# Linear attention in front of a two-layer gated network: attention sums in column halves, shorter weight split, and an engine order set by a planner

## Chip, cores and metric

One core of one Trainium2 chip runs the whole program in one launch. The metric is device time in microseconds, the median of repeated executions; lower is better.

## What is computed

```python
# attention: batch 4, heads 4, seq 1088, head_dim 32, r = 8
phi(x)[i*8+j] = (S1 @ x)[i] * (S2 @ x)[j]          # 64 features of a token and head
kv  = sum over s of phi(k[s]) x v[s]               # 64 x 32 of a batch and head
z   = sum over s of phi(k[s])
x   = (phi(q) @ kv) / (phi(q) @ z + 1e-6)          # 4352 tokens x 128 channels
# gated network: d_model 128, d_ff 2048
h = x @ w_in
g = where(h >= 1, h, where(h <= -1, 0, (h + 1)**2 / 4))
out = g @ w_out
```

The inputs are float64 or float32 arrays; the weights and S arrive as 64-bit words and are turned to float32 parts on the chip.

## The kernel before

**Network.** The 4352 tokens lie in the free dimension in 9 chunks, eight of 512 and one of 256; a *unit* is one chunk with one of 16 blocks of 128 hidden channels, 144 units in all. `up(u)` (L257) forms h in three matmuls (L262 to L264): each operand is a high part that TensorE's one-pass fp32r format holds and a low part that is the remainder, and hi·hi, hi·lo and lo·hi are summed in PSUM. ScalarE makes `s = ((h+1)/2)^2` (L270, L271), VectorE `g = min(max(h,1),s)` (L275), and once more with a rounded output as `g_hi` (L274), or ScalarE rounds a copy (L277, a share of 0.5 of the first 32 units, 0.35 later); GpSimd subtracts for `g_lo` (L278). `down(u)` (L282), four units later, adds three matmuls to the chunk's sum (L289 to L291).

**Attention.** A batch has 9 tiles of 128 tokens, in groups of 3. `features` (L155) projects a group by S (L160, plain fp32, which TensorE runs as two instructions a matmul), copies one factor (L164, ScalarE) and multiplies (L165, VectorE). `k_steps` (L172) sums keys: for each tile and pair of heads, a matmul with 128 stationary feature columns and 66 moving ones (L187: two heads' values and a column of ones for z). `q_steps` (L194) transposes the features (L206), multiplies by kv (L213: 128 stationary columns, 66 moving, which gives numerator and denominator token by token), divides (L219 to L221), and transposes x back to channels (L226) for x_hi and x_lo (L235, L236).

**Weights.** `from_double` (L76) splits 512 columns at a time, eight times: bounds (L82), magnitude (L85), bit moves (L87, L89), range test (L91), exponent (L94), low word as float (L101), its scaling (L102), rounding (L103), remainder (L104) and sum (L105).

**Order.** Attention steps come from generators in two hand-written strings (FS, SS, L26); the main loop (L344) issues as many as the next chunk needs and one more each unit, so attention runs as far ahead as one step a unit takes it. All PSUM tiles share one ring of eight banks (L54). The framework's scheduler, run with a timeline model, then orders each engine's queue.

## Time and profile before

| what | value |
|---|---|
| timed runs, median of 3 (lowest, highest) | 282.64 us (282.19, 283.64) |
| profiled execution, span (no other time of it is listed) | 423.2 us |
| its TensorE clock, mean | 0.555 of full speed |
| busy in it: PE, DVE, ACT, POOL | 418.1, 222.2, 219.5, 204.7 us |

PE is TensorE's matmuls, DVE VectorE, ACT ScalarE, POOL GpSimd, SP the engine that issues DMAs here. The page gives busy time by engine over the span, a strip of 40 slices (PEclk is the granted TensorE clock in tenths), the chain of work that ended last, and groups of instructions by line. The profiled execution ran at little over half of TensorE's clock and so took half as long again as the timed ones; a busy time of PE has to be scaled by the clock of its stretch before it is set beside the timed median, those of the other engines do not.

### The profile page before, as it was taken

The page shows a single profiled execution, that of the slowest core. Times are in us where ns is not written, and L with a number is a line of the kernel's source. Part 1 is how long each engine was busy: PE and PEld are TensorE (multiplying, and loading weights), DVE is VectorE, ACT ScalarE, POOL GpSimd, SP SyncE. Part 2 cuts the span into 40 slices and gives each one's busy share as a digit, 9 for nine tenths or more (in the row PEclk, how much of TensorE's full clock was granted, in tenths as well). Part 3 has the DMA queues.
Part 4 walks back from the last instruction along what each step waited for, and adds up shares of the span by engine and source line. Part 5 has one row for each costly group of instructions (what it writes and reads, how often), then busy time and mean ns, then how long its engine had stood idle before and what let it go on. Part 6 is the DMA issues. An engine that isn't in the chain of part 4 may idle for free.

```text
span 423.2 us, 4212 instructions
## 1 busy us (share of the span) xinstructions
PE 418.1 (99%) x1413; PEld 290.9 (69%) x1413; DVE 222.2 (53%) x390; ACT 219.5 (52%) x422; POOL 204.6 (48%) x173
## 2 busy tenths in 40 slices
PE   8999999999999999999999999999999999999997
PEld 6997877778766767786767655555555555567775
...
PEclk6555555555555555555555555555555555555555
...
GB/s 269 415 163 71 52 57 0 2 57 0 0 2 0 0 51 1 1 2 0 0 25 2 0 0 25 2 1 1 25 2 0 0 25 0 2 25 1 2 1 37
DMA packets 4629, 13.90 MB, mean 33 GB/s; under 512 B 512, under 2 KB 1152, under 8 KB 4608
## 3 DMA queue, kind: packets, MB, share of 16 engines
...
q14 instruction: 10, 0.08, 0.1%
...
## 4 chain that ended last, share of the span: by engine, by line
PE 97%; DMA 1%; DVE 0%; SPq 0%; ACT 0%; issue 0%; ACTq 0%
PE h L264 13%; PE h L262 13%; PE h L263 13%; PE acc L291 12%; PE acc L289 12%; PE acc L290 12%; PE kv L187 6%; PE nd L213 5%; PE tp L206 3%; PE ab_q L160 3%; PE ab_k L160 2%; PE xt L226 2%; DMA q_sb<-in_qT 1%; SPq L113 0%; DVE kp L165 0%; DVE topw L91 0%
## 5 line engine op out<-in xcount | busy, mean ns | idle before, releaser
L278 POOL TENSOR_TENSOR g_lo<-g,g_hi 128x512 fp32r<-128x512 f32 (+1 forms) x140 | 173.1, 1250 | 179.7 <-ACT g_hi L277 108.4
L270 ACT ACTIVATE s<-h 128x512 f32<-128x512 f32 (+1 forms) x144 | 82.3, 574 | 148.9 <-PE h L264 148.2
L274 DVE SCALAR_TENSOR_TENSOR g_hi<-h,s 128x512 fp32r<-128x512 f32 (+1 forms) x89 | 58.0, 651 | 95.5 <-ACT s L271 55.1
L275 DVE SCALAR_TENSOR_TENSOR g<-h,s 128x512 f32<-128x512 f32 (+1 forms) x144 | 92.8, 653 | 27.5 <-ACT s L271 26.7
L271 ACT ACTIVATE s<-s 128x512 f32<-128x512 f32 (+1 forms) x144 | 84.7, 605 | 1.3
L262 PE MATMUL h<-x_hi,wi_hi 128*128 128x512 f32 (+1 forms) x144 | 82.4, 572 | 0.4 <-ACT x_hi L235 0.4
L289 PE MATMUL acc<-g_hi,wo_lo 128*128 128x512 f32 (+1 forms) x144 | 81.4, 566 | 0.0
L264 PE MATMUL h<-x_hi,wi_lo 128*128 128x512 f32 (+1 forms) x144 | 80.6, 560 | 0.0
L291 PE MATMUL acc<-g_lo,wo_hi 128*128 128x512 f32 (+1 forms) x144 | 80.3, 565 | 0.0
L290 PE MATMUL acc<-g_hi,wo_hi 128*128 128x512 f32 (+1 forms) x144 | 79.5, 552 | 0.0
L263 PE MATMUL h<-x_lo,wi_hi 128*128 128x512 f32 (+1 forms) x144 | 79.5, 552 | 0.0
L290 PEld LDWEIGHTS acc<-g_hi,wo_hi 128*128 128x128 f32 x144 | 33.5, 232 | 17.4 <-issue 8.4
L289 PEld LDWEIGHTS acc<-g_hi,wo_lo 128*128 128x128 f32 x144 | 33.3, 231 | 17.3 <-issue 8.6
L291 PEld LDWEIGHTS acc<-g_lo,wo_hi 128*128 128x128 f32 x144 | 33.2, 232 | 16.7 <-issue 8.6
L264 PEld LDWEIGHTS h<-x_hi,wi_lo 128*128 128x128 f32 x144 | 31.2, 216 | 19.6 <-issue 12.0
L262 PEld LDWEIGHTS h<-x_hi,wi_hi 128*128 128x128 f32 x144 | 33.9, 236 | 15.5 <-issue 7.1
L263 PEld LDWEIGHTS h<-x_lo,wi_hi 128*128 128x128 f32 x144 | 32.9, 228 | 16.6 <-issue 10.4
L277 ACT CAST g_hi<-g 128x512 fp32r<-128x512 f32 (+1 forms) x55 | 32.8, 596 | 10.6 <-DVE g L275 10.6
L187 PEld LDWEIGHTS kv<-v_sb,kp 128*128 128x128 f32 x144 | 30.3, 298 | 2.4 <-issue 0.8
L213 PEld LDWEIGHTS nd<-kv_sb,qpT 128*128 128x128 f32 x144 | 29.1, 289 | 3.5 <-issue 1.5
L187 PE MATMUL kv<-v_sb,kp 128*128 128x66 f32 x144 | 29.1, 363 | 0.0
L213 PE MATMUL nd<-kv_sb,qpT 128*128 128x66 f32 x144 | 28.4, 348 | 0.0
...
## 6 DMA issues: line engine op xcount, KB each, us to landing
...
```

The costliest lines, as they stand in the source:

```text
L187: nc.tensor.matmul(kv[:, p * VC : (p + 1) * VC], lhsT=kp[:, t, p * P : (p + 1) * P], rhs=v_sb[:, t, p * VC : (p + 1) * VC], start=(t == 0) ...
L213: nc.tensor.matmul(nd[:, c : c + VC], lhsT=qpT[:, p, i * P : (i + 1) * P], rhs=kv_sb[b][:, p].rearrange("p h c -> p (h c)"), start=True, s ...
L262: nc.tensor.matmul(h[:, :n], lhsT=wi_hi[:, fj], rhs=x_hi[:, :n], start=True, stop=False)
L263: nc.tensor.matmul(h[:, :n], lhsT=wi_hi[:, fj], rhs=x_lo[:, :n], start=False, stop=False)
L264: nc.tensor.matmul(h[:, :n], lhsT=wi_lo[:, fj], rhs=x_hi[:, :n], start=False, stop=True)
L270: nc.scalar.activation(s[:, :n], h[:, :n], AF.Relu, bias=0.5, scale=0.5)
L271: nc.scalar.activation(s[:, :n], s[:, :n], AF.Square)
L275: nc.vector.scalar_tensor_tensor(out=g[:, :n], in0=h[:, :n], scalar=1.0, in1=s[:, :n], op0=ALU.max, op1=ALU.min)
L278: (nc.vector if u >= len(units) - 4 else nc.gpsimd).tensor_tensor(out=g_lo[:, :n], in0=g[:, :n], in1=g_hi[:, :n].bitcast(F32), op=ALU.subt ...
L289: nc.tensor.matmul(acc[:, :n], lhsT=wo_lo[:, fj], rhs=g_hi[:, :n], start=(j == 0), stop=False)
L290: nc.tensor.matmul(acc[:, :n], lhsT=wo_hi[:, fj], rhs=g_hi[:, :n], start=False, stop=False)
L291: nc.tensor.matmul(acc[:, :n], lhsT=wo_hi[:, fj], rhs=g_lo[:, :n], start=False, stop=(j == NJ - 1))
```

## The change

It does five things.

1. *Column halves.* Key sums (new L423) take 64 columns of v as stationary operand and 128 feature columns as moving one, and write PSUM partitions 0 to 63 for one pair of heads and 64 to 127 for the other. Numerators (new L497) take 64 columns of the transposed kv as stationary and up to 384 tokens as moving operand, again into two halves. x so comes out channel by channel, and the transposes of L226 go.
2. *Denominator.* z is summed as an 8x8 matrix a head from the factors (new L406), masked (L411) and multiplied into S2 (L413, L415), so that the query projection gets 32 further columns (L452: 96 instead of 64). VectorE forms the denominator from them (L460, L464), inverts it (L466) and scales one query factor by it (L469) before the features are formed (L473).
3. *Weights by bits.* The low word's three bits are shifted into the float32 pattern (new L332), which replaces L94, L101, L102 and L105 for the weights; GpSimd takes six of the eight bounds (L306).
4. *Buffers.* PSUM is split into rings of 4 (h), 2 (attention) and 2 (sums); x_hi and x_lo are whole arrays.
5. *Order.* Each step states a due unit, an engine (or two), a cost, what it reads and writes; `Plan.run` plays the engines forward in time by these costs, each taking the ready step with the earliest due, none more than 9 units ahead of the earliest step still open, and the framework keeps that order. Attention of a batch is due just before its first chunk.

```diff
-    ps = ctx.enter_context(tc.tile_pool(name="ps", bufs=8, space=PSUM))
+    rings = dict(h=4, at=2, acc=2, k=2, q=2, v=2, raw=3, hc=2, mag=3, m=2, low=1, ab=2, kp=1, as_=2, den=2,
+                 ap=2, qp=2, qpT=4, kvm=1, kvb=2, zm=1, s=4, g=4, g_hi=6, g_lo=6, o=2)
+    ctx.enter_context(tc.manual_schedule())
...
-        nc.vector.tensor_scalar(out=m, in0=top.bitcast(I32), scalar1=-0x00800000, scalar2=None,
-                                op0=ALU.bitwise_and)
-        nc.scalar.activation(low, lw.bitcast(U32), AF.Copy, scale=2.0**-52)
-        nc.gpsimd.tensor_tensor(out=low, in0=low, in1=m.bitcast(F32), op=ALU.mult)
-        nc.scalar.copy(dst_hi, top)
-        nc.gpsimd.tensor_tensor(out=top, in0=top, in1=dst_hi.bitcast(F32), op=ALU.subtract)
-        nc.gpsimd.tensor_tensor(out=dst_lo, in0=top, in1=low, op=ALU.add)
+        plan.either(due, [("DVE", fast(n), None, [raw_tok], [hc], lambda: bound(nc.vector)),
+                          ("POOL", 0.1 + 0.0016 * n, None, [raw_tok], [hc], lambda: bound(nc.gpsimd))])
+        plan.add(due, "DVE", dve(n), lambda: nc.vector.scalar_tensor_tensor(
+            out=of(m), in0=lw(), scalar=29, in1=of(m),
+            op0=ALU.logical_shift_right, op1=ALU.bitwise_or), r=[raw_tok], w=[m])
+        plan.add(due, "POOL", pool_t(n), lambda: nc.gpsimd.tensor_tensor(
+            out=lo, in0=of(mag), in1=hi.bitcast(F32), op=ALU.subtract), r=[mag, toks[0]], w=[toks[1]])
...
-                nc.tensor.matmul(kv[:, p * VC : (p + 1) * VC], lhsT=kp[:, t, p * P : (p + 1) * P],
-                                 rhs=v_sb[:, t, p * VC : (p + 1) * VC], start=(t == 0), stop=(t == NTL - 1))
+                    nc.tensor.matmul(of(kv)[64 * p : 64 * p + 64, :P], lhsT=of(vb)[:, t, 64 * p : 64 * p + 64],
+                                     rhs=of(kp)[:, t, p * P : (p + 1) * P], start=(t == 0), stop=(t == NTL - 1))
+                    nc.tensor.matmul(of(z)[:HR, :HR], lhsT=of(sbuf)[:, 1, m], rhs=of(sbuf)[:, 0, m],
+                                     start=(t == 0), stop=(t == NTL - 1))
...
-                nc.tensor.matmul(nd[:, c : c + VC], lhsT=qpT[:, p, i * P : (i + 1) * P],
-                                 rhs=kv_sb[b][:, p].rearrange("p h c -> p (h c)"), start=True, stop=True)
-        nc.vector.tensor_scalar(out=den[:, :m], in0=ndv[:, :, D:], scalar1=1e-6, scalar2=None, op0=ALU.add)
-        nc.vector.reciprocal(out=den[:, :m], in_=den[:, :m])
-        nc.vector.tensor_tensor(out=x_sb[:, :n].rearrange("p t (h d) -> p (t h) d", h=H), in0=ndv[:, :, :D],
-                                in1=den[:, :m].broadcast_to([P, m, D]), op=ALU.mult)
-            nc.tensor.transpose(out=xt[:, i * P : (i + 1) * P], in_=x_sb[:, i, :], identity=ident)
+                    nc.tensor.matmul(of(abc)[:, i * 96 : (i + 1) * 96], lhsT=of(qb)[:, t], rhs=pr, start=True, stop=True)
+                out=terms[ti][:, :m, :R], in0=of(a)[:, :m], in1=view()[:, :, 2], op=ALU.mult),
+                out=of(den)[:, :m], in_=terms[ti][:, :m], axis=AX.X, op=ALU.add), r=[("terms", ti)], w=[den])
+                out=of(ap)[:, :m], in0=view()[:, :, 0], in1=of(den)[:, :m].broadcast_to([P, m, R]), op=ALU.mult),
+                    nc.tensor.matmul(of(nd)[64 * p : 64 * p + 64, :nt], lhsT=of(kvb)[:, 64 * p : 64 * p + 64],
+                                     rhs=of(qpT[p])[:, :nt], start=True, stop=True)
...
-    for u in range(len(units)):
-        while ready < c0 + n:
-            advance()
-        up(u)
-        advance()
-        if u >= LAG:
-            down(u - LAG)
+                for s, v, ready in todo[e]:
+                    if s.taken is not None or ready > now + 1e-9 or (e != "SP" and s.due > limit):
+                        continue
+                    k = (s.due, sid[s])
+                    if best is None or k < best[0]:
+                        best = (k, s, v)
+            dues.append(lambda f, e=first_of[c] - 4, l=10: e - l + l * f)
+    order = plan.run()
+    for s in order:
+        s.ways[s.taken][5]()
```

How it moves instructions. First TensorE's queue from the first projection to the first unit (h0): `ab_k`/`abk` and `ab_q`/`abq` are projections of keys and queries of a batch and group, `tp` transposed features, `nd` numerators. Before, from L160 on:

```order
L160 MATMUL ab_k0_6_140<-s_sb_108,k_sb0_94 128x64 x3
L160 MATMUL ab_q0_0_148<-s_sb_108,q_sb0_98 128x64 x3
...
L187 MATMUL kv0_171<-v_sb0_99,kp0_125 128x66 x13
L206 MATMUL tp0_0_0_183<-ident_73,qp0_0_147 128x128 x3
...
L213 MATMUL nd0_1_240<-kv_sb0_172,qpT0_1_203 128x66 x5
L226 MATMUL xt0_0_259<-ident_73,x0_0_235 128x128 x3
...
L226 MATMUL xt0_1_278<-ident_73,x0_1_247 128x128 x3
L262 MATMUL h0_318<-x_hi0_263,wi_hi_121 128x512
```

Now:

```order
L390 MATMUL abk0_2_158<-s_all_92,k0_106 128x64 x3
L406 MATMUL z0_150<-ab0_1_156 32x32 x3
L423 MATMUL kv0_172<-kp0_148,v0_121 64x128 x6
...
L413 MATMUL z0_150<-zm0_191,s_all_92 128x32
...
L452 MATMUL abq0_0_212<-proj0_93,q0_110 128x96 x3
...
L483 MATMUL tp0_0_1_262<-ident_66,qp0_0_251 128x128 x3
L497 MATMUL nd0_0_274<-qpT0_0_0_266,kvb0_236 64x384
L497 MATMUL nd0_0_274<-qpT0_0_1_270,kvb0_236 64x384
...
L390 MATMUL abk1_0_313<-s_all_92,k1_146 128x64 x5
L539 MATMUL h0_327<-x_hi_89,wi_hi_85 128x512
```

The query projections have moved behind the key sums and behind z, 12 numerator matmuls have become 4, and no transposes stand between the numerators and h0.

Then the place on TensorE where attention ends, the last group of batch 3. Before, it stands between units 57 and 60 of 144:

```order
L264 MATMUL h58_1834<-x_hi1536_967,wi_lo_122 128x512
L213 MATMUL nd3_2_1819<-kv_sb3_1331,qpT3_2_1748 128x66 x5
L226 MATMUL xt3_1_1847<-ident_73,x3_1_1777 128x128 x3
L262 MATMUL h59_1856<-x_hi1536_967,wi_hi_121 128x512
...
L226 MATMUL xt3_2_1869<-ident_73,x3_2_1826 128x128 x3
L262 MATMUL h60_1882<-x_hi1536_967,wi_hi_121 128x512
```

Now:

```order
L541 MATMUL h105_2528<-x_hi_89,wi_lo_86 128x512
L578 MATMUL acc3072_2392<-g_lo101_2478,wo_hi_87 128x512
L497 MATMUL nd3_1_2538<-qpT3_1_0_2486,kvb3_1985 64x384
L497 MATMUL nd3_1_2538<-qpT3_1_1_2513,kvb3_1985 64x384
L574 MATMUL acc3072_2392<-g_hi102_2498,wo_hi_87 128x512
L575 MATMUL acc3072_2392<-g_hi102_2498,wo_lo_88 128x512
L497 MATMUL nd3_2_2551<-qpT3_2_0_2494,kvb3_1985 64x320
L497 MATMUL nd3_2_2551<-qpT3_2_1_2520,kvb3_1985 64x320
```

The last numerators have moved from unit 58 to unit 105, so that attention lies among 105 units rather than 59.

## Rows read from the trace of the kernel before

**Rows 1.** The page: span, busy time by engine, and the granted clock by slice.

```profile
span 423.2 us, 4212 instructions
PE 418.1 (99%) x1413; PEld 290.9 (69%) x1413; DVE 222.2 (53%) x390; ACT 219.5 (52%) x422; POOL 204.6 (48%) x173
PEclk6555555555555555555555555555555555555555
```

**Rows 2.** Busy time by stretch: start and end, length, then busy us and instructions of PE, weight loads, DVE, ACT and POOL, the granted clock, DMA share, GB/s.

```profile
0.00:33.50 33.50, 31.61 (x141) 28.34 (x141) 18.12 (x36) 11.46 (x26) 7.16 (x14) 0.57 0.72 272
33.50:60.00 26.50, 26.44 (x106) 22.00 (x106) 24.30 (x37) 16.01 (x34) 19.39 (x16) 0.54 0.22 66
60.00:100.00 40.00, 40.00 (x147) 29.70 (x148) 23.18 (x38) 21.62 (x41) 24.55 (x20) 0.55 0.05 15
100.00:140.00 40.00, 40.00 (x144) 28.44 (x142) 22.19 (x40) 17.98 (x34) 19.29 (x15) 0.56 0.00 0
140.00:180.00 40.00, 40.00 (x150) 29.16 (x148) 19.21 (x34) 19.75 (x36) 15.29 (x12) 0.56 0.04 14
180.00:220.00 40.00, 40.00 (x144) 28.35 (x144) 20.03 (x38) 18.02 (x33) 15.24 (x12) 0.56 0.02 7
220.00:260.00 40.00, 40.00 (x129) 26.01 (x128) 20.51 (x40) 20.96 (x38) 15.52 (x13) 0.56 0.00 0
260.00:300.00 40.00, 40.00 (x105) 22.73 (x104) 19.65 (x33) 23.87 (x43) 24.95 (x20) 0.56 0.02 7
300.00:340.00 40.00, 40.00 (x106) 22.79 (x105) 18.09 (x30) 23.39 (x42) 21.79 (x18) 0.56 0.04 14
340.00:380.00 40.00, 40.00 (x113) 23.73 (x112) 17.01 (x29) 22.46 (x43) 20.44 (x17) 0.56 0.02 7
380.00:423.20 43.20, 40.06 (x146) 29.66 (x144) 19.93 (x42) 24.02 (x56) 21.03 (x21) 0.56 0.03 10
```

**Rows 3.** TensorE's matmuls in order of time: start us, us, then the instructions merged; plain fp32 matmuls are two instructions each.

```profile
4.48 3.69 PE L160 MATMUL ab_k<-s_sb,k_sb 128*128 128x64 f32 x18
8.64 4.10 PE L160 MATMUL ab_q<-s_sb,q_sb 128*128 128x64 f32 x18 [0.47 <-DMA q_sb<-in_qT]
12.54 5.76 PE L187 MATMUL kv<-v_sb,kp 128*128 128x66 f32 x26
20.76 2.13 PE L206 MATMUL tp<-ident,qp 128*128 128x128 f32 x9
33.56 0.79 PE L262 MATMUL h<-x_hi,wi_hi 128*128 128x512 f32 x1 [0.35 <-ACT x_hi L235]
...
250.79 0.56 PE L264 MATMUL h<-x_hi,wi_lo 128*128 128x512 f32 x1
251.19 0.56 PE L262 MATMUL h<-x_hi,wi_hi 128*128 128x512 f32 x1
```

**Rows 4.** Groups by line, engine and shape: count, busy us, mean ns, idle time before and its releasers.

```profile
L94 DVE TENSOR_SCALAR mw<-topw 128x512 int32<-128x512 int32 x8 | 6.1, 757 | 0.0
L221 DVE TENSOR_TENSOR x<-nd,den 128x384 f32<-128x384 f32 x12 | 6.7, 556 | 0.3
L219 DVE TENSOR_SCALAR den<-nd 128x12 f32<-128x12 f32 x12 | 2.0, 170 | 13.2 <-PE nd L213 13.0
L236 DVE TENSOR_TENSOR x_lo<-xt,x_hi 128x64 fp32r<-128x64 f32 x4 | 0.9, 216 | 0.0
L236 DVE TENSOR_TENSOR x_lo<-xt,x_hi 128x128 fp32r<-128x128 f32 x3 | 0.9, 284 | 0.0
L274 DVE SCALAR_TENSOR_TENSOR g_hi<-h,s 128x512 fp32r<-128x512 f32 x77 | 53.0, 688 | 93.8 <-ACT s L271 53.5 <-PE acc L290 27.1 <-ACT g_hi L277 5.4
L277 ACT CAST g_hi<-g 128x512 fp32r<-128x512 f32 x51 | 31.2, 612 | 10.3 <-DVE g L275 10.3
L101 ACT ACTIVATE loww<-raw_i 128x512 f32<-128x512 uint32 x4 | 2.7, 663 | 0.0
L102 POOL TENSOR_TENSOR loww<-loww,mw 128x512 f32<-128x512 f32 x8 | 10.2, 1281 | 28.9 <-DVE mw L94 28.9
L104 POOL TENSOR_TENSOR topw<-topw,wi_hi 128x512 f32<-128x512 f32 x4 | 5.1, 1279 | 0.0
L105 POOL TENSOR_TENSOR wi_lo<-topw,loww 128x512 fp32r<-128x512 f32 x4 | 5.8, 1442 | 0.2
```

**Rows 5.** Single lines of VectorE's weight work: count, then shortest, median and longest duration in ns.

```profile
L82 DVE TENSOR_SCALAR hcw<-raw_i x4: 418/419/1500, 12.6 to 53.5; 128x512 f32<-128x512 f32 x4
L89 DVE SCALAR_TENSOR_TENSOR mw<-hcw,mw x8: 679/1086/1655, 13.8 to 101.5; 128x512 int32<-128x512 int32 x8
```

**Rows 6.** Stretches between changes of the granted clock, columns as in Rows 2.

```profile
7.20:24.20 17.00, 16.53 (x79) 16.34 (x79) 8.01 (x13) 5.61 (x14) 2.32 (x2) 0.50 1.02 405
34.50:51.50 17.00, 17.00 (x73) 13.88 (x73) 16.23 (x26) 11.43 (x23) 10.96 (x9) 0.56 0.22 67
51.60:58.40 6.80, 6.80 (x25) 6.03 (x25) 5.82 (x9) 2.61 (x7) 5.81 (x6) 0.50 0.29 89
95.90:99.30 3.40, 3.40 (x13) 2.81 (x13) 1.19 (x2) 1.74 (x3) 3.00 (x3) 0.50 0.00 0
```

**Rows 7.** TensorE just before and in the stretch from 51.60, columns as in Rows 3.

```profile
47.72 4.68 PE L187 MATMUL kv<-v_sb,kp 128*128 128x66 f32 x24
52.20 1.48 PE L160 MATMUL ab_q<-s_sb,q_sb 128*128 128x64 f32 x6
```

More of the change, by code (lines that the diff above doesn't have):

```diff
@@ L241, in woven @@
[L241 to L254 removed]
+    x_hi = cst.tile([P, NT], F32R, name="x_hi")
+    x_lo = cst.tile([P, NT], F32R, name="x_lo")
@@ new lines, in tile_kernel, with heat, emit, load @@
+    SC = S.shape[1]
+    s_raw = cst.tile([P, SC, 2], I32, name="s_raw")
+    s_all = cst.tile([P, SC], F32, name="s_all")
+    proj = [cst.tile([P, H, 3 * R], F32, name=f"proj{i}") for i in range(2)]
+    def heat(due, n):
+        b = bank(f"heat{due}", "h")
+        def emit():
+            for _ in range(n):
+                nc.tensor.matmul(of(b), lhsT=ones[:, :P], rhs=ones, start=True, stop=True)
+        plan.add(due, "PE", n * 0.43, emit, w=[b])
+    def load(due, src, b, size, tok=None, view=lambda t: t):
+        plan.add(due, "SP", 0.5, lambda: nc.sync.dma_start(view(of(b)) if isinstance(b, Buf) else view(b), src),
+                 w=[tok or b], lat=size / 410e3)
@@ new lines, in unit @@
+        plan.add(u, "DVE", dve(n), lambda: clamp(g), r=[h, s], w=[g])
+        if int((u + 1) * 0.36) > int(u * 0.36):
+            plan.add(u, "ACT", act(n, False), lambda: nc.scalar.copy(of(g_hi)[:, :n], of(g)[:, :n]), r=[g], w=[g_hi])
+        else:
+            plan.add(u, "DVE", dve(n), lambda: clamp(g_hi), r=[h, s], w=[g_hi])
+        late = u >= len(units) - 4
+        eng = nc.vector if late else nc.gpsimd
+        plan.add(u, "DVE" if late else "POOL", dve(n) if late else pool_t(n), lambda: eng.tensor_tensor(
+            out=of(g_lo)[:, :n], in0=of(g)[:, :n], in1=of(g_hi)[:, :n].bitcast(F32), op=ALU.subtract),
+            r=[g, g_hi], w=[g_lo])
@@ new lines, in tile_kernel @@
+    heat(-30, 9)
+    load(-30, S, s_raw, P * SC * 8, tok="s_raw")
+    load_attn(0, -29, -28, -27)
+    from_double(-25, lambda: s_raw, "s_raw", SC, "s", whole=s_all, whole_tok="s_all")
+    for i in range(2):
+        plan.add(-20, "ACT", act(64, False), lambda i=i: nc.scalar.copy(
+            proj[i][:, :, : 2 * R], s_all[:, :64].rearrange("p (h c) -> p h c", h=H)), r=["s_all"], w=[("proj", i)])
+    kvb = keys(0, lambda f: -16 + 7 * f)
+    queries(0, kvb, [lambda f: -9 + 4 * f, lambda f: -8 + 4 * f, lambda f: -2 + 5 * f])
@@ new lines, in tile_kernel @@
+    first_unit = {}
+    for u, (c0, n, j) in enumerate(units):
+        first_unit.setdefault(j // JW, u)
+    for c in range(DFF // WC):
+        weights(first_unit[c] - 6 if c else -10, w_in, c, wi_hi, wi_lo, "i")
+        weights(first_unit[c] - 2 if c else -6, w_out, c, wo_hi, wo_lo, "o")
+    need = {}
+    for b in range(1, B):
+        c_first = (b * SEQ) // CH * CH
+        need[b] = first_of[c_first]
+        k0 = 8 if b == 1 else need[b - 1] + 2
+        k1 = need[b] - 18
+        load_attn(b, k0 - 12, k0 - 8, k0 - 10)
+        kvb = keys(b, lambda f, k0=k0, k1=k1: k0 + (k1 - k0) * f)
+        dues = []
+        for gi in range(len(GRP)):
+            tok = b * SEQ + GRP[gi][0] * P
+            c = tok // CH * CH
+            dues.append(lambda f, e=first_of[c] - 4, l=10: e - l + l * f)
+        queries(b, kvb, dues)
```

654 lines of the change are left out of this document (413 added, 241 removed).

## The prediction

> **What bounds the kernel now.** I read the page first, then busy time by stretch, then TensorE in order of time, then the groups by line. In the profiled execution TensorE is busy 418.1 of 423.2 us, and its granted clock stays by the lower of its two levels, 1.2 of 2.4 GHz (mean 0.555) [rows 1]. Nothing else matters there. But the timed median is 282.64, so the timed runs cannot have had that clock: TensorE's 418.1 us at 0.555 are 232 us at the full clock, and to end in 282.64 it needs a mean of at least 232/282.64 = 0.82. I therefore read the profile for durations, scale TensorE's by its clock and leave the others as they are. The profiled span is half as long again as the median, and the sum below is made twice: for the timed clock, which the forecast is for, and for the profiled one, as a check.
>
> At the full clock TensorE is no longer alone. Of each stretch the reader is to take the longest of PE busy x PEclk, DVE, ACT and POOL [rows 2]. From 33.5 to 60 it is DVE (24.3 us, against PE's 26.44 x 0.54 = 14.3), to 100 POOL (24.6), over the four 40 us stretches to 260 PE (40 x 0.555 = 22.2 each; in the first DVE has as much), then POOL (25.0), ACT (23.4, 22.5, 24.0). Their sum is 232.5. PE alone makes 213.9 of these 390 us (14.3 + 22.0 + 320.06 x 0.555), DVE 204.1, ACT 208.1, POOL 197.5. So 18.6 us of the floor are unevenness: while weights and attention are made DVE is full, later it idles and ACT and POOL are full.
>
> The first 33.5 us I keep as they are, since there the clock was at 0.50 although TensorE was busy 16.53 of 17 us [rows 6]: that stretch does not look like one that the timed clock would shorten. With it the floor is 266.0; the median stands 16.6 above, so the part behind the front takes 249.1/232.5 = **1.071** times its floor. That is waiting by order. (If the front did shorten to some 22 us in the timed runs, the factor would be 1.12, and the forecast would come out within 2 us of what follows.)
>
> **TensorE.** Its plain fp32 instructions cost their stationary columns plus twice their moving ones, one after the other: key sums took 5.76/26 = 0.22 us at the lower level, 266 cycles, for 128 + 132 columns; projections 3.69/18 = 0.205, or 246, for 128 + 128; transposes 2.13/9 = 0.24 [rows 3]. At the full clock, over the whole kernel: key sums, 144 instructions of 260 cycles, are 15.6 us; as 144 of 64 + 256 they are 19.2 one after another and 9.6 if the two halves run side by side. Numerators were 15.6 too; as 32 instructions of 64 + 768 and 16 of 64 + 640 cycles they are 15.8, or 7.9 side by side. 36 transposes of x go (-3.8). Query projections gain 64 cycles in 72 instructions (+1.9), z adds 72 of some 96 cycles (+2.9), masks and transposed kv some 0.5. Side by side: -6.0 - 7.7 - 3.8 + 5.3 = **-12.2**; one after another **+5.3**. The trace has no half-width matmul, so both ends stay; I take side by side, because in the network a 512-column matmul starts every 0.40 us with its 128-column load hidden [rows 3], so TensorE does overlap work of neighbouring instructions where they don't need the same cells. Three quarters fall behind the front: -9.2, so PE 204.7 (or 217.9).
>
> The Trainium skill (TensorE: Matmul & The Clock Gate, part 3) says that a weight load overlaps running matmuls only when the row group differs; both halves here use all rows, and by that rule the sum would be nearer the second end. The same part tells of three column tiles running 2.38 times as fast, which is the first end; no run here shows either yet.
>
> **VectorE.** Removed: eight L94 (6.1), six bounds of 0.42 (2.5), L219 (2.0), L221 (6.7) [rows 4, 5]; x in whole groups saves seven x_lo pieces and nine casts with 1536 columns, by 0.216 us at 64 and 0.284 at 128 columns some 0.15 an instruction and 0.00106 a column [rows 4]: 4.0; three fewer key products 0.5. Together -21.8. Added: eight L332 on 512 integers, like L89, 0.68 to 1.66, median 1.09 [rows 5]: 8.7; 36 small instructions of 96 columns, between 0.216 and 0.284, at 0.25: 9.0; g_hi six times more at 512, twice less at 256: 3.3; S with 192 columns and masks: 2. Together +23.0. Net **+1.2** (ends -2 and +6): 205.3 behind the front.
>
> **ScalarE and GpSimd.** ACT loses eight L101 of 0.66 (5.3) and a net 2.9 of roundings (0.612 each), gains 1.6 of x_hi and 2.5 of small copies: **-4.1**, 204.0. POOL's 24 weight instructions of 1.28 to 1.44 become 8 [rows 4], -21; six bounds come, for which no row exists, between DVE's 0.42 and POOL's 1.28, at 1.1: +6.6; **-14**, 183.5. A POOL instruction beside DVE's is not free: the same bound took DVE 0.42 or 1.50 us [rows 5]; that is inside DVE's upper end.
>
> **DMA.** S grows threefold, q and v of batch 0 come in thirds; total bytes hardly change, and behind the first 60 us the DMA share is at most 0.05 [rows 2], so it costs only the 1 us in S's chain, below.
>
> **Front.** Before, h0 starts at 33.56 [rows 3]. Now TensorE has before h0, at the lower level: keys 18 x 0.205 = 3.7, z 36 x 0.08 = 2.9, key sums 36 x 0.267/2 = 4.8, queries 18 x 0.267 = 4.8, 12 transposes 2.8, 8 numerator instructions of 0.69, halved, 2.8, ten projections of batch 1 2.1: 23.9. It starts about 1 us later than 4.48, since seven instructions on S have three times the columns. 29.4, so I take 29. What is late next is the chain of small VectorE instructions ahead of the transposes; it lies beside the key sums of the same batch only in part, and two more us there are in the range.
>
> **Order.** Attention now ends at unit 105, not 58. PE, DVE and ACT then have 204.7, 205.3 and 204.0: perfectly even, the floor would be 205.3, with the old unevenness 223.9. I take the middle, 214.6, since weights must still be made early, where DVE was full (16.23 of 17 us [rows 6]). With the old factor, 214.6 x 1.071 + 29 = **259**; the two ends 249 and 269. At the profiled clock TensorE alone counts: 423.2 - 4.5 - 9.2/0.555 = 402.
>
> **Rivals.**
> 1. *The halves take turns.* PE behind the front 217.9, front 36.6: (217.9 + 9.3) x 1.071 + 36.6 = 280. For it: in plain fp32 load and matmul already run one after the other [rows 3]. Chance 0.13.
> 2. *Each change of shape empties the array.* The new queue changes stationary width 55 times, 42 of them behind the front. A matmul of 0.56 us with the next start after 0.40 [rows 3] has 0.16 still to run; 42 x 0.16 = 6.7 on PE: (211.4 + 9.3) x 1.071 + 31 = 267. The Trainium skill (TensorEngine Tiling (Array Packing), key properties) says that changing the tiling mode drains TensorE; no run here shows it. Chance 0.11.
> 3. *The clock: slower.* After 24 instructions of key sums and six of projections the clock stood at 0.50 for 6.8 us, network matmuls included [rows 6, 7]. Attention behind the front comes in 15 groups (9 of queries, 6 of keys), in half-width matmuls. If each brought 6.8 us at the lower level in a run that otherwise has the upper, PE would need 15 x 3.4 = 51 more: 255.7 x 1.071 + 29 = **303**. It passes 282.64 from 9.4 of the 15 groups on ((282.64 - 29)/1.071 - 204.7 = 32). Against it: behind 34.5 us the old kernel, with 18 such groups, fell twice [rows 6], and the new ones are shorter. Chance 0.09; some other hold-up of a fixed queue, 0.04.
> 4. *The planner does not even out.* 269, with the other gains whole. Chance 0.11.
> 5. *The planner also removes the waits.* 214.6 + 29 = 244, or 234 if even too. Chance 0.12.
>
> **The numbers.** The forecast itself, 249 to 269, has 0.40. What is within 0.5% (281.2 to 284.1) can hardly be told from no change. Faster are the forecast, rivals 2, 4, 5 and half of rival 1: 0.79; slower rival 3, the other hold-up and a third of rival 1: 0.17; the rest 0.04. The range 240 to 281 leaves out rival 3, the low half of rival 5 and the top of rival 1, some 0.2.
>
> **What would show it.** Key sums and numerators: pairs at half their single cost, starts of two halves overlapping. First h about 29 us. Behind the front DVE, ACT and PE x clock each near 205, and no 40 us stretch where one stands 3 us above the others. L332 near 1.1 us. If the granted clock is again 0.56, a span near 402 with PE at 99%; more than 425 there speaks for rival 1. The prediction is wrong at its root if the timed runs are bound by TensorE at a mixed clock: then only TensorE's -12 counts.

## The result

| | median | lowest to highest | runs |
|---|---|---|---|
| before | 283.14 us | 282.19 to 284.93 | 4 |
| after | 274.68 us | 273.26 to 277.12 | 4 |

Ratio 0.969, 95% interval 0.962 to 0.976: faster by 8.5 us, 3.1%. The forecast was 259.0 in 240 to 281. The sign and the range held; of the 23.6 us it promised, about a third came.

The profiled execution of after ran at the full clock behind its front, unlike that of before, so the two pages can't be laid side by side. Its page (span, busy time, granted clock) answers to [rows 1]:

```profile
span 272.7 us, 4152 instructions
PE 256.7 (94%) x1365; PEld 196.8 (72%) x1365; DVE 218.0 (80%) x386; ACT 207.6 (76%) x418; POOL 193.2 (71%) x170
PEclk9997999999999999999999999999999999999999
```

The comparison therefore uses a second profile of the unchanged kernel before (e0 below), which had the upper level for most of its span:

```profile
span 279.6 us, 4212 instructions
PE 266.2 (95%) x1413; PEld 225.1 (81%) x1413; DVE 221.1 (79%) x390; ACT 210.1 (75%) x422; POOL 207.3 (74%) x173
PEclk9757978999999999999999999999999999999999
```

The kernel before was bound by TensorE at the full clock as well: 95% busy. Its busy time is not the 232 us that scaling [rows 1] gave, but 266. Busy time by stretch of after (columns as in [rows 2]) shows where TensorE is the bound and where it isn't:

```profile
20.00:30.00 10.00, 8.35 (x36) 5.09 (x37) 9.03 (x17) 4.59 (x11) 2.33 (x3) 0.83 0.21 57
30.00:40.00 10.00, 9.32 (x44) 6.20 (x42) 10.00 (x15) 9.65 (x22) 7.79 (x6) 1.00 0.18 58
40.00:60.00 20.00, 17.51 (x114) 13.16 (x114) 20.00 (x29) 13.65 (x27) 16.89 (x12) 1.00 0.51 192
60.00:80.00 20.00, 17.00 (x78) 12.02 (x76) 20.00 (x33) 15.48 (x31) 15.97 (x12) 1.00 0.02 6
80.00:100.00 20.00, 20.00 (x109) 15.82 (x108) 18.37 (x33) 17.16 (x34) 17.69 (x14) 1.00 0.15 52
100.00:140.00 40.00, 40.00 (x215) 30.62 (x214) 28.41 (x50) 32.68 (x62) 28.75 (x23) 1.00 0.03 10
...
180.00:220.00 40.00, 40.00 (x193) 31.83 (x192) 33.49 (x63) 35.47 (x68) 32.93 (x27) 1.00 0.04 14
```

From 80 us on TensorE is full, with VectorE, ScalarE and GpSimd below it. From 30 to 80 VectorE is full while weights are split, and TensorE has 6.2 us of idle time. The second profile of before, the same stretches:

```profile
30.00:40.00 10.00, 6.97 (x39) 5.86 (x39) 9.06 (x14) 5.97 (x14) 7.32 (x6) 0.89 0.24 81
40.00:60.00 20.00, 20.00 (x110) 17.28 (x110) 20.00 (x30) 14.89 (x31) 16.69 (x13) 0.88 0.19 61
60.00:80.00 20.00, 19.54 (x118) 16.35 (x117) 19.96 (x34) 16.40 (x33) 19.82 (x14) 1.00 0.09 30
80.00:100.00 20.00, 18.57 (x111) 15.87 (x111) 19.27 (x34) 13.28 (x26) 20.00 (x16) 1.00 0.00 1
```

**What a matmul costs.** The ends of matmuls are modelled in the profile and hide gaps, so I go by their starts. After, in order of time (columns as in [rows 3]): network matmuls, then a burst of key sums and a group of numerators.

```profile
92.17 0.39 PE L574 MATMUL acc<-g_hi,wo_hi 128*128 128x512 f32 x1
92.39 0.39 PE L575 MATMUL acc<-g_hi,wo_lo 128*128 128x512 f32 x1
92.62 0.39 PE L539 MATMUL h<-x_hi,wi_hi 128*128 128x512 f32 x1
92.85 0.39 PE L540 MATMUL h<-x_lo,wi_hi 128*128 128x512 f32 x1
...
106.96 1.31 PE L423 MATMUL kv<-kp,v 128*64 128x128 f32 x20
108.20 0.50 PE L539 MATMUL h<-x_hi,wi_hi 128*128 128x512 f32 x1
108.54 0.40 PE L540 MATMUL h<-x_lo,wi_hi 128*128 128x512 f32 x1
...
135.79 0.39 PE L578 MATMUL acc<-g_lo,wo_hi 128*128 128x512 f32 x1
136.11 0.87 PE L497 MATMUL nd<-qpT,kvb 128*64 128x384 f32 x4
136.91 0.50 PE L574 MATMUL acc<-g_hi,wo_hi 128*128 128x512 f32 x1
```

And in the second profile of before:

```profile
33.17 0.39 PE L263 MATMUL h<-x_lo,wi_hi 128*128 128x512 f32 x1
33.40 0.40 PE L264 MATMUL h<-x_hi,wi_lo 128*128 128x512 f32 x1
33.64 0.39 PE L263 MATMUL h<-x_lo,wi_hi 128*128 128x512 f32 x1
...
118.41 2.12 PE L187 MATMUL kv<-v_sb,kp 128*128 128x66 f32 x18
120.33 0.48 PE L291 MATMUL acc<-g_lo,wo_hi 128*128 128x512 f32 x1
```

Among its like, a network matmul of 512 columns starts 0.227 us after the one before it in after and 0.232 us in before (medians at the full clock); one of 256 columns takes 0.12 in both. Why they are 4 to 5 ns further apart in before is not shown. At the full clock 512 columns alone are 512/2400 = 0.213, so 14 to 19 ns come on top of each. With 768 of the one and 96 of the other the network is **186 us** of TensorE at after's price, 190 at before's. Key sums took 1.92/18 = 0.107 us an instruction before and 1.24/20 = 0.062 now: the halves do run side by side.

Added up start to start behind the first unit (at 33.2 us before, 28.4 after), with network matmuls of both kernels at after's price (0.2275 and 0.121) and what exceeds it apart:

| us of TensorE | before | after |
|---|---|---|
| network at 0.2275 and 0.121 | 185.9 | 185.9 |
| attention | 40.9 | 34.1 |
| above the network's price: waits, returns from attention, lower clock | 16.3 | 20.6 |
| sum | 243.1 | 240.6 |

So it took 4.8 us less in the front and 2.5 less behind it: attention gave 6.8, and 4.3 of that went again into what exceeds the price. Gaps alone (the next instruction starts over 0.13 us later than the price of a network matmul, at the full clock) grew from 5.0 to 10.0 us.

The granted clock has a part in this too. Before's was at 0.50 for 6.8 us behind its first unit, from 37.8 to 44.6; the network matmuls there lie 1.8 us above their price, and 3.4 us of attention ran at half speed, some 3.5 us lost in all (an estimate from these figures). After has no such stretch. At the same clock after would have gained nothing behind the front in these two profiles: what attention gave there, the gaps took. All five profiles of before and its variants at the upper level (e0, e6, e10, e11, e12) have such a stretch; of the ten of after and its variants, eight have none but for the last 2 us, and e1 and e7 have 6.8 us.

The waits of TensorE in after from 28 to 80 us (us in total, times, longest) have one main name, VectorE:

```profile
PE acc L574 <- DVE g_hi L554: 2.3, 2, 1.4
PE h L540 <- DVE x_lo L503: 1.4, 1, 1.4
PE h L539 <- DVE g_hi L554: 1.2, 1, 1.2
PE z L413 <- DVE zm L411: 1.1, 1, 1.1
```

### The profile page after: what moved, and what is told of

Its sections match the earlier page's. It is cut to its first block, busy times and chain, and to the rows that moved or that the text cites. A ratio compares the mean times of both kernels' runs of the same rounds, so it can differ in the third digit from the quotient of the medians.

```text
span 272.7 us, 4152 instructions
## 1 busy us (share of the span) xinstructions
PE 256.7 (94%) x1365; PEld 196.8 (72%) x1365; DVE 218.0 (80%) x386; ACT 207.6 (76%) x418; POOL 193.2 (71%) x170
## 3 DMA queue, kind: packets, MB, share of 16 engines
q1 hardware_dynamic: 5184, 13.70, 14.1%
## 4 chain that ended last, share of the span: by engine, by line
PE 70%; DVE 15%; ACT 9%; issue 3%; DMA 1%; DVEq 0%
PE acc L578 10%; PE acc L574 10%; PE h L539 9%; PE acc L575 9%; PE h L541 8%; PE h L540 8%; ACT s L551 4%; ACT s L549 3%; DVE g L554 3%; PE nd L497 3%; PE abk L390 3%; PE tp L483 3%; PE kv L423 3%; DVE g_hi L554 3%; PE abq L452 2%
## 5 line engine op out<-in xcount | busy, mean ns | idle before, releaser
L539 PE MATMUL h<-x_hi,wi_hi 128*128 128x512 f32 (+1 forms) x144 | 56.9, 395 | 2.4 <-DVE g_hi L554 1.7
L574 PE MATMUL acc<-g_hi,wo_hi 128*128 128x512 f32 (+1 forms) x144 | 56.8, 395 | 2.3 <-DVE g_hi L554 2.3
L540 PE MATMUL h<-x_lo,wi_hi 128*128 128x512 f32 (+1 forms) x144 | 54.7, 380 | 1.4 <-DVE x_lo L503 1.4
L578 PE MATMUL acc<-g_lo,wo_hi 128*128 128x512 f32 (+1 forms) x144 | 54.2, 401 | 1.6 <-DVE g_lo L564 0.9
L541 PE MATMUL h<-x_hi,wi_lo 128*128 128x512 f32 (+1 forms) x144 | 54.6, 379 | 0.0
L575 PE MATMUL acc<-g_hi,wo_lo 128*128 128x512 f32 (+1 forms) x144 | 54.3, 380 | 0.0
L483 PE MATMUL tp<-ident,qp 128*128 128x128 f32 x72 | 12.1, 288 | 1.8 <-DVE qp L473 1.7
L397 DVE TENSOR_TENSOR kp<-ab,abk 128x768 f32<-128x768 f32 (+2 forms) x9 | 10.9, 1214 | 3.3 <-ACT ab L395 3.3
L483 PEld LDWEIGHTS tp<-ident,qp 128*128 128x128 f32 x72 | 9.2, 147 | 6.0 <-issue 1.8
L390 PEld LDWEIGHTS abk<-s_all,k 128*128 128x128 f32 x72 | 10.7, 226 | 3.5 <-DVE s_all L329 1.9
```

The source lines that it names most:

```text
L483: nc.tensor.transpose(out=of(tp)[:, i * P : (i + 1) * P], in_=of(qp)[:, i, p * P : (p + 1) * P], identity=ident)
L539: nc.tensor.matmul(t[:, :n], lhsT=wi_hi[:, fj], rhs=x_hi[:, xs], start=True, stop=False)
L540: nc.tensor.matmul(t[:, :n], lhsT=wi_hi[:, fj], rhs=x_lo[:, xs], start=False, stop=False)
L541: nc.tensor.matmul(t[:, :n], lhsT=wi_lo[:, fj], rhs=x_hi[:, xs], start=False, stop=True)
L574: nc.tensor.matmul(of(acc)[:, :n], lhsT=wo_hi[:, fj], rhs=of(g_hi)[:, :n], start=first, stop=False)
L575: nc.tensor.matmul(of(acc)[:, :n], lhsT=wo_lo[:, fj], rhs=of(g_hi)[:, :n], start=False, stop=False)
```

## The experiments

The theories, as they stand in the texts on record: **A**, TensorE's own price (0.2275 us a matmul) bounds nearly all of the time and order is worth little; **B**, the forecast's, 7% of the time is waiting by order and an even load pays; **C**, the start from 28 to 80 us is bound by VectorE's weight work; **D**, early attention gives TensorE work while the network waits for weights. Experiments on the changed kernel are held against its 274.84 us (ratio 0.967 to before), on the kernel before against the 283 to 285 us that it took beside them.

**e0 and a1: both kernels unchanged.**

> The kernel before, unchanged, for a trace at the full clock. Theory A (TensorE's own price): 512-column network matmuls start 0.2275 us apart as they do after the change, not 0.211 as I scaled them, and TensorE is busy over 90% of the span of about 280 us, with under 10 us idle behind the first unit. Theory B (waiting by order, the forecast's): they start 0.21 us apart and TensorE stands idle for some 17 us or more behind the first unit. If the clock is near 0.55 again, neither is told apart.

> The changed kernel, unchanged, to have its ratio to the kernel before on the chip of the variants beside it: 0.97, 273 to 277 us.

Measured: before 281.81 us in the run that left the second profile shown above; after 274.84 (274.17 to 278.48, 8 runs), ratio 0.967 (0.962 to 0.973). Before's own spacing, 0.232, is not quite the 0.2275 that A named, but far from B's 0.21, and TensorE was 95% busy: this decides for A.

**e2: one of six network matmuls left out** (g_lo·wo_hi, so that product is missing from the output).

```diff
-                ...wo_lo[:, fj], rhs=of(g_hi)[:, :n], start=False, stop=False)
+                ...wo_lo[:, fj], rhs=of(g_hi)[:, :n], start=False, stop=last)
-        plan.add(u + AFTER + 0.01, "PE", rounded(n), down_lo, r=[g_lo], w=[acc])
```

> The changed kernel without the sixth matmul of each unit (g_lo by wo_hi), so the output lacks that product; GpSimd still forms g_lo. It takes 128 matmuls of 512 and 16 of 256 columns, 31 us of TensorE, away. Theory A: TensorE bounds from 80 us on, so 20 to 28 us less (247 to 255), until VectorE (218 us busy) bounds. Theory B, waiting by order: 10 us less or nothing, with TensorE idle for the rest.

Measured: 253.72 us, ratio 0.894 (0.889 to 0.898), 21 us less. 144 matmuls at these prices are 128 x 0.2275 + 16 x 0.121 = 31 us; two thirds of it came through. VectorE and GpSimd keep nearly all their work here, so TensorE is what bounds most of the time, as A expected.

**e4: the halves made to take turns.** Both halves of the key sums write the same partitions.

```diff
-                    nc.tensor.matmul(of(kv)[64 * p : 64 * p + 64, :P], ..., start=(t == 0), stop=(t == NTL - 1))
+                    q = 64 * p if t == NTL - 1 else 0
+                    nc.tensor.matmul(of(kv)[q : q + 64, :P], ..., start=(p == 0 and t == 0) or q > 0, stop=(t == NTL - 1))
```

> The changed kernel with the key sums' two halves writing the same PSUM half (all tiles but the last of a batch), so that they can't run side by side; the sums are not the reference's. If side by side is what made 20 instructions take 1.24 us (0.062 each at the full clock), they now take about 0.133 each: 10 us more of TensorE in all, 7.5 behind the first unit. Theory A (TensorE bounds): 7 to 10 us more, 282 to 285. Theory B (waiting by order): 0 to 3 more, the rest hidden.

Measured: 277.86 us, ratio 0.982 (0.977 to 0.987), 3 to 4 us more, between the two expectations. The burst that stood at 106.96 in after:

```profile
107.05 2.40 PE L424 MATMUL kv<-kp,v 128*64 128x128 f32 x20
109.38 0.50 PE L541 MATMUL h<-x_hi,wi_hi 128*128 128x512 f32 x1
```

20 instructions now take 2.33 us, 0.117 each against 0.062 (and against the 0.133 expected). Start to start, key sums grow from 10.1 to 18.4 us, 5.2 of it behind the first unit; 1.8 us less above the network's price took some back. Side by side is real and worth what TensorE saves, less what VectorE holds it up for anyway.

**e1: rounding of g moved to ScalarE in the start.**

```diff
-        if int((u + 1) * 0.36) > int(u * 0.36):
+        f = 0.7 if u < 36 else 0.3
+        if int((u + 1) * f) > int(u * f):
```

> The changed kernel with ScalarE rounding 0.7 of g_hi in the first 36 units and 0.3 later, instead of 0.36 throughout. Theory A with a VectorE-bound start: VectorE was busy 50 of 50 us between 30 and 80 us while TensorE lacked 6; twelve clamps of 0.68 (8 us) leave VectorE there, so 3 to 6 us less. Theory B: the planner's order already trades the engines off, no change within 1 us. If ScalarE fills up instead (16 of 20 us there), 0 to 3 us more.

Measured: 274.7 us, ratio 0.968 (0.962 to 0.974): nothing, the figure of B; the 3 to 6 us that a start bound by VectorE would have given back did not come. In its profile the gaps did shrink, from 10.0 to 7.0 us, but the clock was at 0.50 from 49.2 to 52.6 and from 59.4 to 62.8, where network matmuls lie 3.3 us above their price. VectorE was still 19.93 of 20 us busy from 40 to 60, with 23 instructions in place of 29. They had become longer on average; the last section bears on why.

**e5: nearly all weight work taken away.** Chunks 1 to 3 are rounded from the upper word by two instructions; their lower bits are left out.

```diff
+        if c:
+            plan.add(due, "ACT", ..., lambda: nc.scalar.copy(hi[:, w], top()), ...)
+            plan.add(due, "POOL", ..., lambda: nc.gpsimd.tensor_tensor(out=lo[:, w], in0=top(), in1=hi[:, w]..., op=ALU.subtract), ...)
+            return
```

> The changed kernel with weight chunks 1 to 3 of each matrix made by two instructions (ScalarE rounds the high word, GpSimd subtracts) instead of seven, so those weights are not the reference's. Takes some 24 VectorE instructions (about 22 us of its busy time) and 6 on GpSimd away between 28 and 80 us. Theory C (the start is bound by VectorE's weight work): TensorE's 10.3 us above its own price there go, 7 to 10 us less. If those waits come from the fixed order, 0 to 3 less.

Measured: 264.4 us, ratio 0.935 (0.929 to 0.940), 9 to 10 us less. TensorE has 20.00 of 20 us from 40 on:

```profile
40.00:60.00 20.00, 20.00 (x120) 15.98 (x119) 12.10 (x27) 16.60 (x33) 18.29 (x15) 1.00 0.29 108
60.00:80.00 20.00, 20.00 (x94) 14.88 (x93) 15.52 (x26) 17.96 (x35) 14.75 (x12) 1.00 0.00 1
```

This is the figure of C: what remained of waiting was weight work, in one place. But the edit takes work from ScalarE and GpSimd too, and e1, which took instructions from VectorE alone, gained no time. So it is shown that weight work holds up the start, not that VectorE's share of it does so alone.

**e7: the changed kernel with the old weight split** (one VectorE instruction L332 out; low word as float on ScalarE, two GpSimd instructions and the exponent on VectorE back in, as L94, L101, L102 and L105 of before).

> The changed kernel with the weight split of the kernel before (the low word as float, scaled, added: one VectorE mask for the shift, one more ScalarE and two more GpSimd instructions a chunk). Part 3 undone. VectorE hardly changes (-8.1 + some 5 us), GpSimd +21, ScalarE +5. If only VectorE bounds the start: 0 to 2 us less or the same. If GpSimd (16 to 17 of 20 us there) fills and holds VectorE up: 3 to 8 us more.

Measured: 281.56 us, ratio 0.995 (0.991 to 0.9996). Without the new split hardly anything of the change is left. From 60 to 100 us GpSimd is full, as the last of the expectations has it, and VectorE is full to 80, with TensorE behind them:

```profile
40.00:60.00 20.00, 17.45 (x110) 13.04 (x109) 20.00 (x32) 16.76 (x33) 19.05 (x15) 1.00 0.48 175
60.00:80.00 20.00, 14.67 (x52) 10.51 (x53) 20.00 (x31) 12.26 (x23) 20.00 (x16) 0.83 0.00 1
80.00:100.00 20.00, 18.78 (x86) 13.64 (x84) 14.26 (x27) 15.72 (x30) 19.81 (x16) 1.00 0.10 29
```

In this profile the clock also fell to 0.50 twice between 60 and 80 us, for 6.8 us in all; the network matmuls there take some 3 us more than at the full clock, a part of the loss that is not the split's own work. And four of the eight bounds stay on GpSimd here (3.9 us), so this is not quite the split of before.

**e10 and e12: the new split alone, in the kernel before.**

```diff
+        if dst_lo is not None:
+            nc.vector.scalar_tensor_tensor(out=m, in0=lw, scalar=29, in1=m, op0=ALU.logical_shift_right, op1=ALU.bitwise_or)
+            ...
+            nc.gpsimd.tensor_tensor(out=dst_lo, in0=top, in1=dst_hi.bitcast(F32), op=ALU.subtract)
+            return
```

> The kernel before with one part of the change alone: the weights' third word goes in by bits (one more VectorE instruction in place of one, one ScalarE and two GpSimd instructions less per chunk). If the parts add up (the changed kernel with the old split was 7 to 8 us slower): 7 to 8 us less than before, 275. If the parts only work together (before, TensorE has 20.0 of 20 us from 40 to 60 with its early attention, so there is little to be gained there): 0 to 3 us less. By the forecast's sum (TensorE not touched, GpSimd -21, VectorE +1): 0 to 4 less.

Measured: 284.39 us, ratio 1.001 (0.998 to 1.005): nothing. So the parts' times don't add up: the change without the split gives 0.5%, the split alone none, both together 3.1%. Its trace:

```profile
30.50:50.50 20.00, 15.85 (x54) 13.32 (x55) 19.71 (x35) 8.96 (x21) 9.01 (x7) 0.50 0.26 83
60.00:80.00 20.00, 20.00 (x117) 17.10 (x116) 19.74 (x33) 16.05 (x33) 17.08 (x13) 1.00 0.07 24
80.00:100.00 20.00, 20.00 (x126) 17.57 (x125) 12.78 (x27) 12.96 (x24) 11.67 (x10) 1.00 0.02 8
```

From 60 to 100 the split did its work, GpSimd at 28.75 in place of 39.82; TensorE, which has attention there in this kernel, had only 1.9 us of idle time to gain (38.11 of 40 before), and took it. Behind the first unit its gaps at the full clock fell from 5.0 to 0.8 us. What took this back in the profile is the granted clock: it stands at 0.50 from 30.4 to 50.9 us, 20.5 us against 6.8 behind before's front, and network matmuls there start 0.427 us apart in place of 0.232. Those in that stretch lie 6.7 us above their price, in before 1.8, and 6.5 us of attention ran at the lower clock against 3.4. Why the clock stayed down is not shown. A second profile was to show the split at another course of the clock:

> A second look at the kernel before with the new split alone, whose first profile had the clock at 0.50 for 20 us from 30.5 to 50.5, against 7 us in the kernel before's. If that stretch hides a gain of the split, a run with a shorter one ends 3 to 5 us earlier, 278 to 280; if TensorE's load with attention hides it, the span stays within 2 us of 282.5 whatever the clock.

Measured: 285.0 us, span 283.2, at 0.50 from 10.7 to 51.7 us. Behind the front the clock was no different, so this profile does not show the split without it.

**e11: the light weights of e5, in the kernel before.** The edit is that of e5 in `make_weights`; the lower bits of chunks 1 to 3 are left out.

> The kernel before with the weights of chunks 1 to 3 rounded from the upper word by two instructions (their lower bits are left out): nearly all weight work behind the front falls away from VectorE, ScalarE and GpSimd; the order and attention stay. In the changed kernel the same was worth 10 us. If the start of the kernel before is full on TensorE with attention (from 33 to 100 us its trace has 35 us of network, 22 of attention and some 6 of waits): 2 to 5 less, 279 to 282. If it is held by weight work as the changed kernel's start is: 8 to 12 less, 272 to 276. If the lower clock behind the front is what keeps the time up, the profile has 7 us or more at 0.50 there and the time falls by no more than 3.

Measured: 277.54 us, ratio 0.978 (0.971 to 0.984), 6 to 7 us less, between the first two expectations. The start of the kernel before is held by weight work too, less than that of the changed kernel (9 to 10): its gaps were 5.0 us to begin with, those of after 10.0, and attention filling TensorE's holes is the likely reason. The gaps that are left are 0.8 us, as in e10. But here the clock behind the front is at 0.50 only from 31.4 to 38.2:

```profile
30.00:40.00 10.00, 9.07 (x42) 7.76 (x42) 4.17 (x12) 5.30 (x11) 5.02 (x4) 0.66 0.17 52
```

So in the kernel before the split removes as many gaps as light weights do, and the lower clock, not a lack of gaps, is what separates e10's nothing from e11's 6 to 7 us in these profiles.

**e6: the kernel before with attention spread out.** One attention step in 0.6 of the units, so that it ends about unit 95 instead of 58: evenness alone.

```diff
-        advance()
+        if share(u, 0.6):
+            advance()
```

> The kernel before with one change: in three of five units one attention step is issued ahead instead of in every unit, so that attention ends near unit 95 instead of 60. Evenness alone. Forecast's theory (18.6 us of unevenness): 5 to 10 us less. Theory A (TensorE full in nearly every stretch at 0.2275 a matmul): within 2 us of the kernel before.

Measured: 289.83 us, ratio 1.025 (1.017 to 1.033): 7 us more, which neither expectation had. The stretches from 30 to 60:

```profile
30.00:40.00 10.00, 5.82 (x37) 4.40 (x35) 9.21 (x16) 6.06 (x14) 7.22 (x6) 0.93 0.24 86
40.00:60.00 20.00, 18.72 (x85) 15.49 (x85) 19.21 (x26) 11.88 (x24) 14.75 (x12) 0.78 0.21 67
```

TensorE's busy time from 30 to 100 falls from 65.08 to 61.99 us, with VectorE and GpSimd nearly as full as before. This fits D: early attention had not been a burden on the start but TensorE's work while it waits for weights. Not all of the 7 us is that: gaps grew by 2.2 us, and the clock was at 0.50 for 10.2 us behind the front in place of 6.8, which costs some 2 more by the estimate made above for before.

**e9: the opposite, the changed kernel with attention packed** (due times behind unit 32 compressed to 0.45; it ends about unit 65).

```diff
+    PACK = lambda u: u if u < 32 else 32 + 0.45 * (u - 32)
-        need[b] = first_of[c_first]
+        need[b] = PACK(first_of[c_first])
-            dues.append(lambda f, e=first_of[c] - 4, l=10: e - l + l * f)
+            dues.append(lambda f, e=PACK(first_of[c] - 4), l=10: e - l + l * f)
```

> The changed kernel with attention earlier: the due times behind unit 32 are compressed to 0.45, so the last numerators stand ahead of unit 65 instead of 106. The forecast's theory (even load pays): 4 to 10 us more than the changed kernel. Theory A (TensorE's own price, order hardly matters): within 2 us. Theory D, from the kernel before with its attention spread out, which was 7 us slower (early attention gives TensorE work while the network waits for weights): 1 to 4 us less; but VectorE is full to 80 us here, and if that decides, 2 to 6 us more.

Measured: 278.01 us, ratio 0.977 (0.970 to 0.984), 3 us more. VectorE is at 20.00 of 20 us in both stretches to 80 anyway, and attention's VectorE work now stands among the weights'. The last expectation named this; D's 1 to 4 us less did not come. The interval overlaps that of the unchanged after (0.962 to 0.973), so the loss is at the edge of the noise; what is clear is that packing gains nothing.

**e3: the changed kernel without the fixed order** (the framework's scheduler orders the same instructions).

```diff
-    ctx.enter_context(tc.manual_schedule())
```

> The changed kernel without the line that fixes the order: the framework's scheduler interleaves the same instructions. Theory A (behind the first unit 186 of the 241 us are TensorE's own price of the network, 34 that of attention, and only some 10 us between 28 and 80 us are a wait, for VectorE's weight work): within 3 us of the changed kernel's 274.8, since another order neither shortens TensorE's own work nor VectorE's. The forecast's theory (7% of the time is waiting by order, which an order can cause or remove): 5 to 15 us more or less.

Measured: 278.51 us, ratio 0.980 (0.974 to 0.986), 3 to 4 us more, a little over A's bound and under B's 5 to 15. The planner's order is worth that much.

**e8: no range tests on the weights.** Weights beyond float32's range would come out wrong; the rest is computed in full.

```diff
+        if lo is not None:
+            ...tensor_scalar(out=of(m), in0=raw()[:, :, 1], scalar1=0x07FFFFFF, scalar2=3, ...)
+            ...
+            return
```

> The weights are split without the range tests (no bound, no absolute value, no zeroing of what is too small for float32; numbers outside the float32 range would come out wrong): per chunk a bound of some 0.85 us on GpSimd, an absolute value on ScalarE and one VectorE instruction of 1.04 us fall away, over eight chunks 8.3 us of VectorE and 6.8 of GpSimd. Theory C (between 28 and 80 us TensorE waits for VectorE's weight work; with nearly all of that work taken from six chunks the time fell by 10): 4 to 7 us less than the changed kernel, 268 to 271. The forecast's theory (even load, waits by order): 8.3/2 x 1.071 = 4 us less at most if spread over everything, and the same 20 us stretches with VectorE full. If VectorE's instructions only stretch to fill the time, as when ScalarE took g_hi: no change.

Measured: 267.76 us, ratio 0.944 (0.937 to 0.952), 7 us less than the changed kernel: the fastest version that computes the whole product, at the price of inputs it can't take. TensorE from 60 to 80 rises from 17.00 to 19.68 of 20, VectorE falls to 17.73. It is C's figure once more, with the same reserve as in e5: GpSimd lost work as well.

## Why the prediction was right in sign and wrong in size

**What bounds the kernel: failed, and it is the step that costs most.** The prediction scaled TensorE's busy time by the profile's clock to 213.9 us behind the front and took the longest engine of each stretch, so that in six of ten stretches another engine than TensorE stood as the bound. In that profile a network matmul started 0.384 us after the one before (mean), which is what 512 columns take at 0.555 of the clock; scaled, it is 0.213. The 14 to 19 ns that come on top at the full clock stand in no row at the lower one. At after's price before has 185.9 + 40.9 = 227 us of TensorE behind the first unit, at its own 230: 13 to 16 us more than the sum had, and TensorE was full nearly everywhere. The prediction named this root itself ("bound by TensorE ...: then only TensorE's -12 counts"); that is what happened, at a mean clock of 0.93 to 0.99 listed for the timed runs of before. -12.2 in all would have given 270.4, 4 us under the measured time.

**The factor 1.071: failed, as a consequence.** The 16.6 us above the floor were called waiting by order. In the second profile of before the gaps behind the first unit are 5.0 us; the rest of what lies above TensorE's price is small costs at the ends of bursts, the lower clock and the wider spacing. e3, e6 and e9 show other orders to cost 3 to 7 us (e9 at the edge of the noise, e6 with some of it due to the clock); none gained.

**Order and evenness: failed.** Of the forecast's 23.6 us, halving the unevenness is 10.0 (223.9 to 214.6, times 1.071), the load taken off full stretches 9.2 (232.5 to 223.9), the front 4.5. But TensorE was full nearly everywhere, so evening out the others had nothing to give; e6, evenness alone, lost 7 us. Behind the first unit 2.5 us came in place of 19, no more than before had lost there at the lower clock. That the sign held rests on the front and on this, and was in part luck; that the range held is owed to its width.

**TensorE's instructions: right in sum.** Forecast -12.2 side by side; measured start to start over the whole kernel, attention fell from 68.9 to 54.4 us, -14.5 (some of before's front at the lower clock). By term: key sums 19.9 to 10.1, numerators 16.8 to 10.7, transposes of x 3.8 to 0, queries +1.2 for +1.9, z +5.1 for +2.9. Behind the first unit -6.8 for -9.2. z was the mis-sized term: put at 72 x 0.04, it took 3.8 us start to start, and the product with the masked matrix 1.3 more.

**Rival 1 and the rule of the Trainium skill.** The halves overlap: 0.062 against 0.117 when forced to take turns (e4), 1.9 times as fast. Even taking turns they cost less than the 0.133 that 64 stationary and twice 128 moving columns one after the other make by the prediction's own formula, so its +5.3 was too dear. The Trainium skill (TensorE: Matmul & The Clock Gate, part 3) would let a load overlap only when the row group differs; both halves use all rows here, and the trace disagrees. With its 2.38 for three column tiles the trace agrees in kind.

**Rival 2: real, and small.** The first matmul after any attention burst starts the next one 0.32 us later instead of 0.23 (120.33 to 120.65 in before, a 128-wide burst). That is 0.09 a return, some 62 returns before and 55 after behind the first unit: no loss by the change. What the change adds is at narrower bursts (64 or 32 columns or 32 rows): the matmul ahead of one is held to 0.32 (135.79 to 136.11 above), 0.318 to 0.328 in 17 of the 18 such cases (in the other TensorE waits), against 0.23 ahead of a 128-wide burst (118.18 to 118.41 in before). Leaving costs 0.02 more than leaving a wide one (108.20 to 108.54). The trace has 48 changes of shape behind the front, for the prediction's 42, so this makes some 2.5 us, not 6.7. The Trainium skill (TensorEngine Tiling (Array Packing), key properties) says that changing the tiling mode drains TensorE; the trace agrees, at 0.09 us on the way in.

**Rival 3: did not happen.** After's record has 0.50 for 3.4 us, in the front (and up to 13.5 us, where the record begins, pairs of key sums start 0.213 us apart, twice their later 0.109); behind the front none. Before is the one whose clock falls there, by the account above some 3.5 us that no term of the sum had:

```profile
37.80:44.60 6.80, 6.80 (x27) 6.12 (x26) 6.76 (x10) 4.72 (x11) 3.20 (x3) 0.50 0.48 161
```

**Rivals 4 and 5.** Neither as priced: the load stayed uneven (VectorE full to 80 us), and what TensorE loses above its price grew from 16.3 to 20.6 instead of going.

**VectorE, ScalarE, GpSimd: GpSimd right in size, wrong in worth.** Busy time fell by 3.1, 2.5 and 14.1 us (forecast +1.2 with ends -2 and +6, -4.1 and -14); VectorE's is outside its ends, but holds waiting too, as the last section shows. The rows of after that answer to [rows 4, 5]:

```profile
L332 DVE SCALAR_TENSOR_TENSOR mo<-raw_o,mo 128x512 int32<-128x512 int32 x4 | 4.3, 1081 | 0.0
L306 POOL TENSOR_SCALAR hco<-raw_o 128x512 f32<-128x512 f32 x3 | 2.6, 853 | 0.7 <-ACT magi L311 0.7
L464 DVE TENSOR_REDUCE den<-terms 128x12 f32<-128x108 f32 x12 | 2.9, 256 | 0.1
```

L332 was put at 1.09, the bounds at 1.1 (too dear), small operations at 0.25. Yet the -14 on GpSimd, entered as off the path, belongs to the part that turned out to be worth most: with the old split (e7) some 7 of the 8.5 us are gone.

**Front: right, within what one profile can tell.** 29 forecast; in after the first h starts at 26.2 us and units run on from 28.4, in the second profile of before from 31.3 and 33.2. In a second profile of after (a1) the first h starts at 29.1: there pairs of key sums start 0.213 us apart for as long as they last. So the front moves by 3 us with the clock.

**The chances.** Those of a faster kernel add up to 0.80, not 0.79.

Still open: why the clock falls behind the front in some orders and not in others, and so what the split alone is worth in the kernel before; whether VectorE or GpSimd is the one that holds up the start; and what the clock did in the timed runs, for which only a mean is listed.

## What to carry to other kernels

A profile at the lower clock can't be scaled to the upper one: count matmuls and get their start-to-start spacing at the clock the timed runs have, before anything is called waiting. If the bound engine is full nearly everywhere, even load and a better order have nothing to give; look for the one stretch where it isn't, and for what is full there. The times of parts need not add up: test each one alone and each one removed, and look at the granted clock behind the front before a part that gains no time is called worthless.

## What the runs showed beyond that

VectorE's time for an instruction depends on GpSimd's beside it. In after, VectorE in order of time (columns as in [rows 3]):

```profile
52.99 1.51 DVE L306 TENSOR_SCALAR hci<-raw_i 128x512 f32<-128x512 f32 x1
54.43 1.51 DVE L312 TENSOR_SCALAR mo<-hco 128x512 int32<-128x512 int32 x1
55.87 0.41 DVE L312 TENSOR_SCALAR mi<-hci 128x512 int32<-128x512 int32 x1
```

and GpSimd:

```profile
52.75 1.48 POOL L339 TENSOR_TENSOR wi_lo<-magi,wi_hi 128x512 fp32r<-128x512 f32 x1
54.18 1.48 POOL L564 TENSOR_TENSOR g_lo<-g,g_hi 128x512 fp32r<-128x512 f32 x1
57.62 1.61 POOL L564 TENSOR_TENSOR g_lo<-g,g_hi 128x512 fp32r<-128x512 f32 x1 [1.96 <-DVE g_hi L554]
```

The same L312 takes 1.51 us while a GpSimd instruction runs, ending 0.28 us after it, and 0.41 while GpSimd is idle. All eight of them in after divide so: 0.40 to 0.42 us in the four with GpSimd idle, 1.12 to 1.52 in the four beside a GpSimd instruction. So VectorE's "20.00 of 20" in the start is partly waiting for GpSimd, which fits e1 (fewer instructions, the same busy time) and e7 (more GpSimd work, TensorE 2.3 us less from 60 to 80), though no run here takes GpSimd's work away alone. The Trainium skill (SBUF — State Buffer, SBUF: two separate sides) says that the two engines share a pair of ports as an exclusive lock, which a VectorE instruction needs in a two-port mode or with two SBUF inputs, and that the loser waits for the whole instruction; the trace agrees on the waiting, and which mode L312 has it does not show.
